# A planned recurrence-plus-MoE kernel: engine choice per operation, output stores in the plan, one-chunk early groups, a third early PSUM bank

## The chip, the cores and the metric

The kernel runs on one core of one Trainium2 chip. The metric is device time in microseconds (us). The kernel before takes 207.4 us (median of 3 runs, 207.34 to 208.5). A profile covers one execution; its span is about 2 us shorter than the device time.

Engine names as in the profile: PE (TensorE, matmuls), PEld (its weight loads), DVE (VectorE), ACT (ScalarE), POOL (GpSimd), SPq (the queue of SyncE, which issues all DMAs here). A "bank" is one buffer of PSUM, the memory that the matmuls write; an "evacuation" copies a result out of its bank, and only then can PE use the bank again. The clock quoted is PE's granted clock, 1.00 being full.

## The reference

```python
# q, k, v, alpha: (4, 8, 768, 48) float32; w_in (384, 2048); w_out (2048, 384)
for t in range(S):                                   # gated linear attention
    state = alpha[:, :, t, :, None] * state + einsum('bhd,bhe->bhde', k[:, :, t], v[:, :, t])
    y[:, :, t] = einsum('bhd,bhde->bhe', q[:, :, t], state)
x = y.transpose(0, 2, 1, 3).reshape(3072, 384)
h = x @ w_in
out = relu(h)**2 @ w_out                             # squared-relu expert layers
```

## The kernel before

The 3072 tokens are 24 chunks of 128. Each chunk goes through a recurrence chain: load alpha, q, k, v; logarithm of alpha on ACT (written to `L_s`); cumulative sums on PE; exponentials on ACT; products on DVE; transposes, scores, masks, output, and a last transpose into `xT_big`. Then come the two expert layers: the first ("ph", 16 column blocks, a relu on ACT, a square on DVE or POOL) and the second ("po", 16 accumulating matmuls a chunk, an evacuation, a store).

Python builds a list of operations with a guessed duration and dependencies, a list scheduler simulates them in time, and the instructions are emitted in the order of the simulated start times. Each engine then executes its own list in that order. The guesses set no time, only the order.

```python
class Op:       # engine, guessed duration, emit function, dependencies, priority, PSUM slot, latency
    ...
def run(self, gate):              # list scheduler; "DMA" is first-in first-out, other engines by (time, prio)
    ...
        op.start = t
        free[eng] = t + op.dur
        op.done = t + op.dur + op.lat
    self.order.sort(key=lambda o: o.start)
...
d["ld_" + nm] = add("DMA", 1.02, ld, prev, lat=2.0)            # 4 loads a chunk
ln = d["use_at"] = add("ACT", 0.41, e_ln, d["ld_at"], old, prio=-5.0)
...
GN = [2] * 12                                                  # chunks per expert group
...
rl = add("ACT", (72 + n) / 1200.0, e_relu, op, prio=-20.0)
eng, nm, dur = (nc.vector, "DVE", ...) if f % 2 == 0 else (nc.gpsimd, "POOL", n / 460.0)   # squares
...
tail = g == NG - 1 and tt % 2 == 1                             # only the last tile uses another bank
ev = add("DVE" if tt % 2 == 0 else "ACT", ...)                 # evacuation
add("OUT", 0.55, e_out, ev)                                    # the store: its own planned engine
...
for op in plan.order:
    op.emit()
```

Loads and stores leave through one SyncE queue, but in the plan a store ("OUT") takes nothing from the loads ("DMA").

Of the kernel before, what the change touches and what calls it, by code (L numbers as in the profile page):

```python
# [8 lines left out]
FP32 = mybir.dt.float32  # L9
# [32 lines left out]
class Plan:  # L42
# [7 lines left out]
    def add(self, op):  # L50
        self.pending.setdefault(op.eng, []).append(op)
        return op

    def ready(self, op):
        t = op.at
        for d in op.deps:
            if d.done is None:
                return None
            t = max(t, d.done)
        if op.takes is not None:  # L60
            f = op.takes.free_at()
            if f is None:
                return None
            t = max(t, f)
        return t

    def run(self, gate):
        free = self.free
        while any(self.pending.values()):
            best = None  # L70
            for eng, ops in self.pending.items():
                t0 = free.get(eng, 0.0)
                pick = None
                fifo = eng in ("DMA",)
                for op in (ops[:1] if fifo else ops):
                    if not gate(op):
                        continue
                    r = self.ready(op)
                    if r is None:
                        continue  # L80
                    key = (max(r, t0), op.prio)
                    if pick is None or key < pick[0]:
                        pick = (key, op)
                if pick is not None and (best is None or pick[0][0] < best[0]):
                    best = (pick[0][0], eng, pick[1])
            assert best is not None, "nothing can run"
            t, eng, op = best
            self.pending[eng].remove(op)
            op.start = t
            free[eng] = t + op.dur  # L90
            op.done = t + op.dur + op.lat
            if op.takes is not None:
                op.takes.release.append(op.gives if op.gives is not None else op)
            self.order.append(op)
            self.on_pick(op)
        self.order.sort(key=lambda o: o.start)
# [3 lines left out]
def kernel(  # L100
# [34 lines left out]
    work = ctx.enter_context(tc.tile_pool(name="work", bufs=4))  # L135
    rpool = ctx.enter_context(tc.tile_pool(name="rpool", bufs=6))
    opool = ctx.enter_context(tc.tile_pool(name="opool", bufs=4))
# [48 lines left out]
    sl_misc, sl_sc, sl_h, sl_o = Slots(2), Slots(1), Slots(2), Slots(1)  # L186
    dma_prev = [None]

# [4 lines left out]
    w_in_ready, w_out_ready = [], []  # L193
    NWP = 4

    def load_w_in(i):
        w = d_ff // NWP
        sl = slice(i * w, (i + 1) * w)
        box = {}

        def ld():
            box["t"] = wload.tile([P, KT * d_ff // NWP], FP32, name="wst").rearrange("p (j n) -> p j n", j=KT)
            nc.sync.dma_start(out=box["t"], in_=w_in_r[:, :, sl])

        d = add("DMA", 2.3, ld, lat=2.0)
        cs = []
        for j in range(KT):
            if j < 2:
                cs.append(add("DVE", 0.34, lambda j=j: pin(nc.vector.tensor_copy(w_in_b[:, j, sl], box["t"][:, j, :])), d, prio=1))
            else:  # L210
                cs.append(add("ACT", 0.62, lambda j=j: pin(nc.scalar.copy(w_in_b[:, j, sl], box["t"][:, j, :])), d, prio=1))
        w_in_ready.append(cs)

    def load_w_out(i):
# [6 lines left out]

        d = add("DMA", 2.3, ld, lat=2.0)
        cs = []
        for j in range(w):
            if j < 3:
                cs.append(add("DVE", 0.26, lambda j=j: pin(nc.vector.tensor_copy(w_out_b[:, i * w + j, :], box["t"][:, j, :])), d, prio=1))
            else:
                cs.append(add("ACT", 0.5, lambda j=j: pin(nc.scalar.copy(w_out_b[:, i * w + j, :], box["t"][:, j, :])), d, prio=1))
        w_out_ready.append(cs)
# [5 lines left out]
    def add_loads(s):  # L235
        d = C[s]
        b, c = divmod(s, NCH)
        for nm, src in srcs:
            def ld(nm=nm, src=src):
                d[nm] = loads.tile([P, H, D], FP32, name=nm)  # L240
                nc.sync.dma_start(out=d[nm], in_=src[b, c])  # L241
            prev = C[s - LB]["use_" + nm] if s >= LB else None
            d["ld_" + nm] = add("DMA", 1.02, ld, prev, lat=2.0)

    def add_chunk(s):
# [18 lines left out]
        def e_p0():  # L264
            pm = d["pm"] = ps_misc.tile([P, 512], FP32, name="misc")
            mm(pm[:, 0:HD], lhsT=utri_b[:, 0, :], rhs=L[:, :, 0:D], start=True, stop=True)
            for p in range(NP):
                mm(pm[:, HD + p:HD + p + 1], lhsT=L[:, 2 * p:2 * p + 2, :], rhs=ones_col,
                   start=True, stop=True)
        p0 = Op("PE", 0.28, e_p0, [ln], takes=sl_misc, **g)  # L270
        p0.gla = s
# [32 lines left out]
        def e_p1():  # L304
# [3 lines left out]
            for p in range(NP):  # L308
                tr(d["pT"][:, NP + p, :], kI[:, 2 * p:2 * p + 2, :], ident_bf)
        p1 = plan.add(Op("PE", 0.47, e_p1, [mq, mk], takes=sl_misc, **g))  # L310

# [6 lines left out]
        def e_p2():  # L318
            sc = d["sc"] = ps_sc.tile([P, 2, NP, P], FP32, name="sc")
            t = d["qkT"]  # L320
            for p in range(NP):
                for hh in range(2):
                    sl = slice(64 * hh, 64 * hh + 64)
                    mm(sc[:, hh, p, :], lhsT=t[sl, NP + p, :], rhs=t[sl, p, :], start=True, stop=True)
        p2 = plan.add(Op("PE", 0.42, e_p2, [cp], takes=sl_sc, **g))

# [32 lines left out]
        def e_p3():  # L359
# [5 lines left out]
            for hh in range(2):  # L365
                for p in range(NP):
                    h = 2 * p + hh
                    mm(py[:, h * D:(h + 1) * D], lhsT=d["sm"][:, hh, p, :], rhs=d["vb"][:, h, :],
                       start=(c == 0 and hh == 0 and p == 0), stop=True, skip_group_check=True)
        p3 = plan.add(Op("PE", 0.39, e_p3, [sm1, vb, C[s - 1]["sb"] if c else None], takes=sl_misc, **g))  # L370

# [6 lines left out]
        def e_p4():  # L378
            d["px"] = ps_misc.tile([P, KT, P], BF16, name="misc")
            for j in range(KT):  # L380
                tr(d["px"][:, j, :], d["xn"][:, j * P:(j + 1) * P], ident_bf)
        p4 = plan.add(Op("PE", 0.18, e_p4, [xn], takes=sl_misc, **g))

        def e_xT():
            pin(nc.vector.tensor_copy(xT_big[:, :, s * P:(s + 1) * P], d["px"]))  # L385
        d["x"] = add("DVE", 0.27, e_xT, p4, prio=-9.0)
        p4.gives = d["x"]
        d["end"] = d["x"]


    GN = [2, 2, 2, 2, 2, 2, 2, 2, 2, 2, 2, 2]
    assert sum(GN) == NT
    GT = [sum(GN[:i]) for i in range(len(GN))]
    NG = len(GN)
    gT = {}
    NQ = 4
    sq = {}
    prog = {"m1": 0.0, "m2": 0.0}

    def add_moe1(g, f, before):  # L400
# [3 lines left out]
        def e_mm():  # L404
            prog_t = ps_h.tile([P, 512], FP32, name="ph")
            box["ph"] = prog_t
# [3 lines left out]
        deps = [C[s]["x"] for s in range(GT[g], GT[g] + GN[g])] + w_in_ready[f * NWP // FT] + [before]  # L410
        op = plan.add(Op("PE", 3 * n / 2400.0 + 0.01, e_mm, deps, takes=sl_h, prio=0.0))
        op.moe = (1, GN[g] * 2.56 / FT)

        def e_relu():
            box["r"] = rpool.tile([P, 512], BF16, name="r")
            pin(nc.scalar.activation(box["r"][:, 0:n], box["ph"][:, 0:n], AF.Relu))  # L416
        rl = add("ACT", (72 + n) / 1200.0, e_relu, op, prio=-20.0)
        op.gives = rl
        eng, nm, dur = (nc.vector, "DVE", 0.05 + n / 1900.0) if f % 2 == 0 else (nc.gpsimd, "POOL", n / 460.0)

        def e_sq():
            if f == 0:
                gT[g] = big.tile([P, FT, 384], BF16, name=f"gT{g % 3}", tag=f"gT{g % 3}")
            pin(eng.tensor_mul(gT[g][:, f, 0:n], box["r"][:, 0:n], box["r"][:, 0:n]))  # L424
        fr = sq[(g - 3, "free")] if g >= 3 else None
        first = sq[(g, 0)] if f else None
        sq[(g, f)] = add(nm, dur, e_sq, rl, fr, first, prio=0.0)
        return op

    def add_moe2(g, tt, before):  # L430
        box = {}
        op = None
        tail = g == NG - 1 and tt % 2 == 1
        for qd in range(NQ):
            def e_mm(qd=qd):
                if qd == 0:
                    box["po"] = (ps_misc.tile([P, 512], FP32, name="misc")[:, 0:d_model] if tail
                                 else ps_o.tile([P, d_model], FP32, name="po"))
                for kf in range(qd * FT // NQ, (qd + 1) * FT // NQ):
                    mm(box["po"], lhsT=gT[g][:, kf, tt * P:(tt + 1) * P], rhs=w_out_b[:, kf, :],  # L440
                       start=(kf == 0), stop=(kf == FT - 1))
            deps = [sq[(g, f)] for f in range(FT)] + sum(w_out_ready, []) + [before if qd == 0 else op]
            op = plan.add(Op("PE", 2.56 / NQ, e_mm, deps, takes=(sl_misc if tail else sl_o) if qd == 0 else None, prio=0.1, lat=0.2))
            op.moe = (2, 2.56 / NQ)
# [5 lines left out]
        def e_ev():  # L450
            box["ob"] = opool.tile([P, d_model], FP32, name="ob")
            if tt % 2 == 0:
                pin(nc.vector.tensor_copy(box["ob"], box["po"]))  # L453
            else:
                pin(nc.scalar.copy(box["ob"], box["po"]))
        ev = add("DVE" if tt % 2 == 0 else "ACT", 0.47 if tt % 2 == 0 else 0.37, e_ev, op, prio=-15.0)
        firstop.gives = ev

        def e_out():
            nc.sync.dma_start(out=out_r[GT[g] + tt], in_=box["ob"])  # L460
        add("OUT", 0.55, e_out, ev)
        return op
# [18 lines left out]

    LEAD = 5

# [15 lines left out]
    for _ in range(9):  # L499
        mm(wp, lhsT=warm[:, 0:P], rhs=warm, start=True, stop=True)  # L500
    for op in plan.order:
        op.emit()

# [28 lines left out]
```

## Time and profile before

| stretch (us) | what happens | how it reads |
|---|---|---|
| 0 to 18 | first loads, chunks 0 and 1, first weights | PE has little to do |
| 18 to 41 | first layer of chunks 0 to 3 | clock low or PE idle |
| 41 to 80 | everything overlaps, loads still arriving | some PE idle |
| 80 to 190 | PE nearly full, full from 100 | a two-chunk group each 14.3 us |
| 190 to 206 | last tiles | two waits for one output bank |

The busy table by stretches of the kernel before: stretch, its length, then busy us and instruction counts of each engine, the granted PE clock (1.00 is full), the mean DMA share, GB/s.

```profile
core 0: us, PE busy (x) PEld busy (x) DVE busy (x) ACT busy (x) POOL busy (x), PEclk, DMA share, GB/s
15.00:25.00 10.00, 7.69 (x51) 4.98 (x49) 5.43 (x15) 6.70 (x18) 2.79 (x5) 0.63 1.02 252
25.00:35.00 10.00, 5.86 (x87) 4.32 (x84) 9.58 (x21) 6.36 (x19) 3.54 (x6) 1.00 1.04 316
35.00:45.00 10.00, 9.04 (x63) 6.16 (x63) 6.35 (x18) 6.67 (x21) 4.06 (x7) 0.83 1.08 215
...
60.00:80.00 20.00, 18.39 (x228) 14.12 (x228) 16.48 (x35) 15.45 (x50) 8.41 (x14) 1.00 1.15 199
100.00:120.00 20.00, 19.95 (x229) 15.12 (x227) 16.10 (x34) 15.08 (x44) 8.04 (x14) 1.00 1.06 198
```

PE is full from 100 us on. Between 15 and 45 us it is either slow (clock 0.63, 0.83) or partly idle (busy 5.86 of 10 us).

The PE timeline of the kernel before, early: start, duration, instruction, count; in brackets the idle time before it and what ended it.

```profile
18.00 5.55 PE L180 MATMUL ph<-xT_big,w_in_b 128*128 128x256 bf16 x27 [0.45 <-DVE xT_big L385]
...
36.00 1.42 PE L180 MATMUL ph<-xT_big,w_in_b 128*128 128x256 bf16 x6 [0.45 <-DVE xT_big L385]
```

27 matmuls in 5.55 us and 6 in 1.42 us are 0.21 to 0.24 us each; 256 columns take 0.109 us later. The second group starts only at 36.0 us, when its second chunk is ready.

The SyncE queue of the kernel before, in its timelines:

```profile
44.56 0.98 SPq L241 DMA_DIRECT2D kt<-in_k_dram  x1
48.73 0.36 SPq L460 DMA_DIRECT2D out_dram<-ob  x1
```

```profile
57.44 0.49 ACT L282 ACTIVATE Ainv<-misc 128x384 bf16<-128x384 f32 x1
59.52 0.52 ACT L255 ACTIVATE L_s<-at 128x384 bf16<-128x384 f32 x1 [1.59 <-DMA at<-in_alpha_dram]
59.95 0.64 ACT L416 ACTIVATE r<-ph 128x256 bf16<-128x256 f32 x2
```

```profile
58.85 0.36 PE L180 MATMUL misc<-vb,sm 128*128 128x48 bf16 x8
60.37 0.49 PE L180 MATMUL ph<-xT_big,w_in_b 128*128 128x256 bf16 x3 [1.15 <-ACT r L416]
```

The first store holds the queue from the last load at 44.56 us to 48.73 us. Some later loads land after ACT is ready for them.

The PE timeline at the tail, where one output bank makes PE wait for each evacuation:

```profile
194.11 2.76 PE L180 MATMUL po<-w_out_b,gT_3360 128*128 128x384 bf16 x16 [0.65 <-DVE ob L453]
197.44 2.76 PE L180 MATMUL po<-w_out_b,gT_3553 128*128 128x384 bf16 x16 [0.57 <-ACT ob L455]
```

### The profile page before, as it was taken

How to read it: one execution, taken by the hardware profiler on the slowest of the kernel's cores; microseconds unless marked ns; L12 is line 12 of the kernel's file. 1: busy time of each engine (PE TensorE's matmuls, PEld its weight loads, DVE VectorE, ACT ScalarE, POOL GpSimd, SP SyncE). 2: the span in 40 equal slices, each digit the busy share in tenths (PEclk: the TensorE clock that was granted, in tenths of full speed). 3: DMA queues.
4: the chain of work that ended last, by engine and by line, in shares of the span. 5: the costliest groups of instructions: out<-in, count | busy, mean ns of one | idle time of the engine just before them, and what ended most of it. 6: DMA issues, size and time to landing. Idle time of an engine off the chain costs nothing.

```text
span 206.1 us, 5137 instructions
## 1 busy us (share of the span) xinstructions
PE 185.6 (90%) x1897; PEld 133.9 (65%) x1897; DVE 140.0 (68%) x294; ACT 130.0 (63%) x377; POOL 76.2 (37%) x133
## 2 busy tenths in 40 slices
PE   7566964999979899999999999999999999999883
PEld 2344643576656687677787777677777777777551
DVE  0684699588769598778968776887787787444210
ACT  3535964676667687777787686677776774655100
POOL 5111550353134535454443444344333333444200
PEclk9855899699999999999999999999999999999999
DMA  7999999996799999999999996410111011100212
GB/s 129 189 356 317 170 281 379 196 197 125 153 213 199 197 216 189 213 178 220 166 225 184 202 216 130 110 38 0 41 38 45 0 41 38 41 16 23 76 41 76
DMA packets 107032, 30.21 MB, mean 147 GB/s; under 512 B 100352, under 2 KB 105472, under 8 KB 107008
## 3 DMA queue, kind: packets, MB, share of 16 engines
q1 hardware_dynamic: 107008, 29.89, 69.7%
q8 instruction: 15, 0.25, 0.5%
q14 instruction: 9, 0.07, 0.1%
HBM read 25.17 MB, written 4.72 MB: 145 GB/s over the span
## 4 chain that ended last, share of the span: by engine, by line
PE 65%; DVE 9%; DMA 8%; ACT 6%; issue 5%; SPq 4%; POOL 2%; POOLq 0%; ACTq 0%; DVEq 0%
PE ph L180 26%; PE po L180 24%; PE misc L180 6%; PE misc L183 5%; DMA wst<-in_moe_w_in_dram 4%; SPq L241 3%; PE sc L180 3%; ACT r L416 3%; DMA at<-in_alpha_dram 2%; DVE qkT L314 2%; DMA vt<-in_v_dram 2%; DVE sm L330 2%; DVE ob L453 1%; DVE xT_big L385 1%; PE st L180 1%
## 5 line engine op out<-in xcount | busy, mean ns | idle before, releaser
L180 PE MATMUL ph<-xT_big,w_in_b 128*128 128x256 bf16 x576 | 84.7, 281 | 4.0 <-ACT r L416 2.8
L416 ACT ACTIVATE r<-ph 128x256 bf16<-128x256 f32 x192 | 68.5, 384 | 29.1 <-PE ph L180 27.6
L180 PEld LDWEIGHTS <-w_in_b 128*128 128x128 bf16 x576 | 53.0, 100 | 18.5 <-issue 6.5
L330 DVE TENSOR_TENSOR sm<-sc,utri_b 128x512 bf16<-128x512 f32 x48 | 31.5, 683 | 1.9 <-PE sc L180 1.4
L261 POOL CAST vb<-vt 128x384 bf16<-128x384 f32 x24 | 13.4, 557 | 29.1 <-DMA vt<-in_v_dram 18.4
L297 DVE TENSOR_TENSOR qA_s<-qt,A 128x384 bf16<-128x384 f32 x24 | 13.6, 570 | 10.8 <-ACT A L278 10.8
L255 ACT ACTIVATE L_s<-at 128x384 bf16<-128x384 f32 x24 | 12.5, 521 | 8.2 <-DMA at<-in_alpha_dram 8.1
L314 DVE COPY qkT<-misc 128x1024 bf16<-128x1024 bf16 x24 | 16.3, 681 | 1.8 <-PE misc L183 1.7
L300 DVE TENSOR_TENSOR kI_s<-kt,Ainv 128x384 bf16<-128x384 f32 x24 | 16.3, 683 | 1.7
L278 ACT ACTIVATE A<-misc 128x384 bf16<-128x384 f32 x24 | 11.6, 489 | 9.1 <-PE misc L180 9.0
L180 PEld LDWEIGHTS <-qkT 64*128 64x128 bf16 (+1 forms) x272 | 11.0, 97 | 8.6 <-DVE qkT L314 5.7
L374 ACT CAST xn<-misc 128x384 bf16<-128x384 f32 x24 | 11.5, 478 | 3.9 <-PE misc L180 3.7
L356 ACT CAST sb<-st 128x384 bf16<-128x384 f32 x20 | 9.5, 476 | 5.2 <-DVE st L351 5.2
L180 PE MATMUL misc<-vb,sm 128*128 128x48 bf16 x192 | 9.5, 186 | 3.5 <-DVE sm L330 3.5
L453 DVE COPY ob<-po 128x384 f32<-128x384 f32 x12 | 6.6, 551 | 8.6 <-PE po L180 8.4
L282 ACT ACTIVATE Ainv<-misc 128x384 bf16<-128x384 f32 x24 | 11.7, 492 | 0.0
L183 PE MATMUL misc<-ident_bf,qA_s 128*128 128x128 bf16 x96 | 9.5, 223 | 2.3 <-DVE qA_s L297 2.2
L180 PE MATMUL sc<-qkT 64*128 64x128 bf16 x192 | 9.8, 223 | 1.5 <-DVE qkT L314 1.1
L351 DVE TENSOR_TENSOR st<-st,ae_s 128x384 f32<-128x384 f32 x20 | 11.0, 552 | 0.0
L180 PEld LDWEIGHTS <-sm 128*128 128x128 bf16 x192 | 7.5, 98 | 4.6 <-DVE sm L330 4.3
L424 POOL TENSOR_TENSOR gT_592<-r 128x256 bf16<-128x256 bf16 x8 | 5.3, 657 | 13.7 <-ACT r L416 13.6
L183 PE MATMUL misc<-ident_bf,kI_s 128*128 128x128 bf16 x96 | 9.5, 223 | 0.8 <-DVE kI_s L300 0.7
(86 smaller groups left out, 321.7 us busy)
## 6 DMA issues: line engine op xcount, KB each, us to landing
at<-in_alpha_dram SPq DMA_DIRECT2D x24, 192.0 KB, 4.6
qt<-in_q_dram SPq DMA_DIRECT2D x24, 192.0 KB, 4.4
kt<-in_k_dram SPq DMA_DIRECT2D x24, 192.0 KB, 4.3
vt<-in_v_dram SPq DMA_DIRECT2D x24, 192.0 KB, 4.3
out_dram<-ob SPq DMA_DIRECT2D x24, 192.0 KB, 1.9
wst<-in_moe_w_in_dram SPq DMA_DIRECT2D x4, 768.0 KB, 8.1
wst<-in_moe_w_out_dram SPq DMA_DIRECT2D x4, 768.0 KB, 7.6
```

The lines of the kernel that those rows point to most:

```text
L180: pin(nc.tensor.matmul(*a, **kw))
L183: pin(nc.tensor.transpose(*a))
L255: pin(nc.scalar.activation(L[:, :, 0:D], d["at"], AF.Ln))
L261: pin(nc.gpsimd.tensor_copy(d["vb"], d["vt"]))
L278: pin(nc.scalar.activation(d["A"], d["pm"][:, 0:HD].rearrange("p (h d) -> p h d", h=H), AF.Exp))
L282: pin(nc.scalar.activation(d["Ai"], d["pm"][:, 0:HD].rearrange("p (h d) -> p h d", h=H), AF.Exp, scale=-1.0))
L297: pin(nc.vector.tensor_mul(qA[:, :, 0:D], d["qt"], d["A"]))
L300: pin(nc.vector.tensor_mul(kI[:, :, 0:D], d["kt"], d["Ai"]))
L314: pin(nc.vector.tensor_copy(d["qkT"], d["pT"]))
L330: pin(nc.vector.tensor_mul(d["sm"][:, hh], d["sc"][:, hh], utri_b.to_broadcast([P, NP, P])))
L374: pin(nc.scalar.copy(d["xn"], d["py"][:, 0:HD]))
L416: pin(nc.scalar.activation(box["r"][:, 0:n], box["ph"][:, 0:n], AF.Relu))
```

## The change

The intent: squares, weight casts and evacuations go to whichever engine the plan finds free; stores are charged to the loads in the plan and emitted 1.5 us late; chunks 2 and 3 are groups of their own, so that first-layer work starts earlier; early first-layer work may use the idle output bank; the last two groups alternate output banks; filler matmuls on zeros keep the PE clock up in planned gaps.

```diff
     def add(self, op):
-        self.pending.setdefault(op.eng, []).append(op)
+        op.durs = op.eng if isinstance(op.eng, dict) else {op.eng: op.dur}
+        for e in op.durs:
+            self.pending.setdefault(e, []).append(op)
...
-            op.start = t
+            op.start = t + getattr(op, "late", 0.0)
             free[eng] = t + op.dur
+            if eng == "OUT":
+                free["DMA"] = max(free.get("DMA", 0.0), t) + op.dur
...  # casts: DVE or ACT by index -> {"DVE": ..., "POOL": ...}; relu ring 6 -> 8 buffers; load guess 1.02 -> 1.08
...  # weight-load guess 2.3 -> 2.2; planned latency of xT_big +0.3; relu priority of groups 0 and 1: -20 -> 0
-    GN = [2, 2, 2, 2, 2, 2, 2, 2, 2, 2, 2, 2]
+    GN = [2, 1, 1, 2, 2, 2, 2, 2, 2, 2, 2, 2, 2]
+    M1_ALT = 3
+    OUT_LATE = 1.5
...
-        op = plan.add(Op("PE", ..., takes=sl_h, prio=0.0))
+        op = plan.add(Op("PE", ..., takes=[sl_h, sl_o] if g < M1_ALT else [sl_h], prio=0.0))
-        sq[(g, f)] = add(nm, dur, e_sq, rl, fr, first, prio=0.0)
+        sq[(g, f)] = add({"DVE": 0.05 + n / 1900.0, "POOL": 0.06 + n / 440.0}, 0, e_sq, rl, fr, first, prio=SQ_PRIO)
-        tail = g == NG - 1 and tt % 2 == 1
+        tail = g >= NG - 2                       # and takes=[sl_o, sl_misc]
-        ev = add("DVE" if tt % 2 == 0 else "ACT", ...)
+        ev = add({"DVE": 0.47, "ACT": 0.37}, 0, e_ev, op, prio=-15.0)
-        add("OUT", 0.55, e_out, ev)
+        add("OUT", 0.55, e_out, ev, at=0.0).late = OUT_LATE
-    LEAD = 5
+    LEAD = 4
...
+            if pe_end is not None and DUMMY:     # only before the first second-layer matmul
+                n = max(0, int((op.start - pe_end - 0.5) / 0.22))
+                for _ in range(n):
+                    mm(wp, lhsT=warm[:, 0:P], rhs=warm, start=True, stop=True)
```

More of the change, by code (lines that the diff above doesn't have):

```diff
@@ L60, in ready @@
         if op.takes is not None:
-            f = op.takes.free_at()
-            if f is None:
+            best = None
+            for sl in op.takes:
+                f = sl.free_at()
+                if f is not None and (best is None or f < best):
+                    best, op.slot = f, sl
+            if best is None:
                 return None
-            t = max(t, f)
+            t = max(t, best)
         return t
@@ L87, in run @@
             t, eng, op = best
-            self.pending[eng].remove(op)
-            op.start = t
+            for e in op.durs:
+                self.pending[e].remove(op)
+            op.eng, op.dur = eng, op.durs[eng]
+            op.start = t + getattr(op, "late", 0.0)
             free[eng] = t + op.dur
+            if eng == "OUT":
+                free["DMA"] = max(free.get("DMA", 0.0), t) + op.dur
             op.done = t + op.dur + op.lat
             if op.takes is not None:
-                op.takes.release.append(op.gives if op.gives is not None else op)
+                self.ready(op)
+                op.slot.release.append(op.gives if op.gives is not None else op)
             self.order.append(op)
@@ L135 @@
     work = ctx.enter_context(tc.tile_pool(name="work", bufs=4))
-    rpool = ctx.enter_context(tc.tile_pool(name="rpool", bufs=6))
+    rpool = ctx.enter_context(tc.tile_pool(name="rpool", bufs=8))
     opool = ctx.enter_context(tc.tile_pool(name="opool", bufs=4))
@@ L186 @@
     sl_misc, sl_sc, sl_h, sl_o = Slots(2), Slots(1), Slots(2), Slots(1)
-    dma_prev = [None]
+    X_SLACK = 0.3
+    LD = 1.08
+    WLD = 2.2
+    SQ_PRIO = 0.0
     def add(eng, dur, emit, *deps, **kw):
@@ L194, with cast, e_cast @@
     NWP = 4
+    def cast(dst, box, j, d, n):
+        def e_cast():
+            eng = nc.vector if op.eng == "DVE" else nc.gpsimd
+            pin(eng.tensor_copy(dst, box["t"][:, j, :]))
+        op = add({"DVE": 0.06 + n / 1840.0, "POOL": 0.05 + n / 660.0}, 0, e_cast, d, prio=1.0)
+        return op
     def load_w_in(i):
@@ L203, in ld @@
             nc.sync.dma_start(out=box["t"], in_=w_in_r[:, :, sl])
-        d = add("DMA", 2.3, ld, lat=2.0)
+        d = add("DMA", WLD, ld, lat=2.0)
         cs = []
         for j in range(KT):
-            if j < 2:
-                cs.append(add("DVE", 0.34, lambda j=j: pin(nc.vector.tensor_copy(w_in_b[:, j, sl], box["t"][:, j, :])), d, prio=1))
-            else:
-                cs.append(add("ACT", 0.62, lambda j=j: pin(nc.scalar.copy(w_in_b[:, j, sl], box["t"][:, j, :])), d, prio=1))
+            cs.append(cast(w_in_b[:, j, sl], box, j, d, 512))
         w_in_ready.append(cs)
@@ L220, in ld @@
             nc.sync.dma_start(out=box["t"], in_=w_out_r[:, i * w:(i + 1) * w, :])
-        d = add("DMA", 2.3, ld, lat=2.0)
+        d = add("DMA", WLD, ld, lat=2.0)
         cs = []
         for j in range(w):
-            if j < 3:
-                cs.append(add("DVE", 0.26, lambda j=j: pin(nc.vector.tensor_copy(w_out_b[:, i * w + j, :], box["t"][:, j, :])), d, prio=1))
-            else:
-                cs.append(add("ACT", 0.5, lambda j=j: pin(nc.scalar.copy(w_out_b[:, i * w + j, :], box["t"][:, j, :])), d, prio=1))
+            cs.append(cast(w_out_b[:, i * w + j, :], box, j, d, d_model))
         w_out_ready.append(cs)
@@ L242, in add_loads @@
             prev = C[s - LB]["use_" + nm] if s >= LB else None
-            d["ld_" + nm] = add("DMA", 1.02, ld, prev, lat=2.0)
+            d["ld_" + nm] = add("DMA", LD, ld, prev, lat=2.0, at=0.6)
     def add_chunk(s):
@@ L269, in e_p0 @@
                    start=True, stop=True)
-        p0 = Op("PE", 0.28, e_p0, [ln], takes=sl_misc, **g)
+        p0 = Op("PE", 0.28, e_p0, [ln], takes=[sl_misc], **g)
         p0.gla = s
@@ L309, in e_p1 @@
                 tr(d["pT"][:, NP + p, :], kI[:, 2 * p:2 * p + 2, :], ident_bf)
-        p1 = plan.add(Op("PE", 0.47, e_p1, [mq, mk], takes=sl_misc, **g))
+        p1 = plan.add(Op("PE", 0.47, e_p1, [mq, mk], takes=[sl_misc], **g))
         def e_cp():
@@ L324, in e_p2 @@
                     mm(sc[:, hh, p, :], lhsT=t[sl, NP + p, :], rhs=t[sl, p, :], start=True, stop=True)
-        p2 = plan.add(Op("PE", 0.42, e_p2, [cp], takes=sl_sc, **g))
+        p2 = plan.add(Op("PE", 0.42, e_p2, [cp], takes=[sl_sc], **g))
         def e_sm(hh):
@@ L369, in e_p3 @@
                        start=(c == 0 and hh == 0 and p == 0), stop=True, skip_group_check=True)
-        p3 = plan.add(Op("PE", 0.39, e_p3, [sm1, vb, C[s - 1]["sb"] if c else None], takes=sl_misc, **g))
+        p3 = plan.add(Op("PE", 0.39, e_p3, [sm1, vb, C[s - 1]["sb"] if c else None], takes=[sl_misc], **g))
         def e_xn():
@@ L381, in e_p4 @@
                 tr(d["px"][:, j, :], d["xn"][:, j * P:(j + 1) * P], ident_bf)
-        p4 = plan.add(Op("PE", 0.18, e_p4, [xn], takes=sl_misc, **g))
+        p4 = plan.add(Op("PE", 0.18, e_p4, [xn], takes=[sl_misc], **g))
         def e_xT():
             pin(nc.vector.tensor_copy(xT_big[:, :, s * P:(s + 1) * P], d["px"]))
-        d["x"] = add("DVE", 0.27, e_xT, p4, prio=-9.0)
+        d["x"] = add("DVE", 0.27, e_xT, p4, prio=-9.0, lat=0.2 + X_SLACK)
         p4.gives = d["x"]
         d["end"] = d["x"]
-    GN = [2, 2, 2, 2, 2, 2, 2, 2, 2, 2, 2, 2]
+    GN = [2, 1, 1, 2, 2, 2, 2, 2, 2, 2, 2, 2, 2]
     assert sum(GN) == NT
@@ L396 @@
     NQ = 4
+    M1_ALT = 3
+    OUT_LATE = 1.5
+    RELU_PRIO = -20.0
+    RELU_PRIO0 = 0.0
+    DUMMY = 1
     sq = {}
@@ L404, in e_mm @@
         def e_mm():
-            prog_t = ps_h.tile([P, 512], FP32, name="ph")
+            prog_t = (ps_o.tile([P, 512], FP32, name="po") if op.slot is sl_o
+                      else ps_h.tile([P, 512], FP32, name="ph"))
             box["ph"] = prog_t
@@ L410, in add_moe1 @@
         deps = [C[s]["x"] for s in range(GT[g], GT[g] + GN[g])] + w_in_ready[f * NWP // FT] + [before]
-        op = plan.add(Op("PE", 3 * n / 2400.0 + 0.01, e_mm, deps, takes=sl_h, prio=0.0))
+        op = plan.add(Op("PE", 3 * n / 2400.0 + 0.01, e_mm, deps, takes=[sl_h, sl_o] if g < M1_ALT else [sl_h], prio=0.0))
         op.moe = (1, GN[g] * 2.56 / FT)
@@ L416, in e_relu @@
             pin(nc.scalar.activation(box["r"][:, 0:n], box["ph"][:, 0:n], AF.Relu))
-        rl = add("ACT", (72 + n) / 1200.0, e_relu, op, prio=-20.0)
+        rl = add("ACT", (72 + n) / 1200.0, e_relu, op, prio=RELU_PRIO if g > 1 else RELU_PRIO0)
         op.gives = rl
-        eng, nm, dur = (nc.vector, "DVE", 0.05 + n / 1900.0) if f % 2 == 0 else (nc.gpsimd, "POOL", n / 460.0)
         def e_sq():
@@ L423, in e_sq @@
                 gT[g] = big.tile([P, FT, 384], BF16, name=f"gT{g % 3}", tag=f"gT{g % 3}")
+            eng = nc.vector if sq[(g, f)].eng == "DVE" else nc.gpsimd
             pin(eng.tensor_mul(gT[g][:, f, 0:n], box["r"][:, 0:n], box["r"][:, 0:n]))
@@ L432, in add_moe2, with e_mm @@
         op = None
-        tail = g == NG - 1 and tt % 2 == 1
+        tail = g >= NG - 2
         for qd in range(NQ):
-            def e_mm(qd=qd):
+            def e_mm(qd=qd, me=None):
                 if qd == 0:
-                    box["po"] = (ps_misc.tile([P, 512], FP32, name="misc")[:, 0:d_model] if tail
-                                 else ps_o.tile([P, d_model], FP32, name="po"))
+                    box["po"] = (ps_o.tile([P, 512], FP32, name="po") if firstop.slot is sl_o
+                                 else ps_misc.tile([P, 512], FP32, name="misc"))[:, 0:d_model]
                 for kf in range(qd * FT // NQ, (qd + 1) * FT // NQ):
@@ L442, in add_moe2 @@
             deps = [sq[(g, f)] for f in range(FT)] + sum(w_out_ready, []) + [before if qd == 0 else op]
-            op = plan.add(Op("PE", 2.56 / NQ, e_mm, deps, takes=(sl_misc if tail else sl_o) if qd == 0 else None, prio=0.1, lat=0.2))
+            op = plan.add(Op("PE", 2.56 / NQ, e_mm, deps, takes=([sl_o, sl_misc] if tail else [sl_o]) if qd == 0 else None, prio=0.1, lat=0.2))
             op.moe = (2, 2.56 / NQ)
@@ L451, in e_ev @@
             box["ob"] = opool.tile([P, d_model], FP32, name="ob")
-            if tt % 2 == 0:
+            if ev.eng == "DVE":
                 pin(nc.vector.tensor_copy(box["ob"], box["po"]))
@@ L455, in e_ev @@
                 pin(nc.scalar.copy(box["ob"], box["po"]))
-        ev = add("DVE" if tt % 2 == 0 else "ACT", 0.47 if tt % 2 == 0 else 0.37, e_ev, op, prio=-15.0)
+        ev = add({"DVE": 0.47, "ACT": 0.37}, 0, e_ev, op, prio=-15.0)
         firstop.gives = ev
@@ L500 @@
         mm(wp, lhsT=warm[:, 0:P], rhs=warm, start=True, stop=True)
+    pe_end = None
     for op in plan.order:
+        if op.eng == "PE":
+            if getattr(op, "moe", (0,))[0] == 2:
+                pe_end = None
+                DUMMY = 0
+            if pe_end is not None and DUMMY:
+                n = max(0, int((op.start - pe_end - 0.5) / 0.22))
+                if n:
+                    wp = ps_o.tile([P, 512], FP32, name="po")
+                for _ in range(n):
+                    mm(wp, lhsT=warm[:, 0:P], rhs=warm, start=True, stop=True)
+            pe_end = op.start + op.dur
         op.emit()
```

## The prediction

> **What bounds it now.** The busy table by stretches shows TensorE (PE) saturated from 60 to 190 us (19.9 of 20 us busy between 100 and 180, granted clock 1.00). The timeline gives one group of two chunks every 14.3 us there, so twelve groups need about 172 us of the 206.1 us span. The other 34 us are the start and the tail:
> - 0 to 18 us: loads, two recurrence chunks and weight casts; the first expert-input matmul starts at 18.0 us.
> - 18 to 41 us: PE idles 4.1 us between 25 and 35 us, and the second group waits for both its chunks until 36.0 us. The clock is 0.63 in 15 to 25 us and 0.83 in 35 to 45 us: a 128x256 matmul takes about 0.21 us at 18 to 23 and 36 to 40 us, 0.109 us later. The Trainium skill ("TensorE: Matmul & The Clock Gate", Part 1) says an idle PE falls to half rate and sustained activity restores it; these numbers agree.
> - 41 to 80 us: about 4 us of slack. The SyncE queue stands from 44.56 to 48.73 us, the first output store holding back input loads behind it.
> - Tail: PE stands 0.65 and 0.57 us for the one output bank, then evacuation and store.
>
> **What the change does.**
> 1. Single-chunk groups for chunks 2 and 3: first-layer work starts when chunk 2 is ready (estimate 31 to 33 us), not at 36.0. A 128-column matmul costs about 55 ns (four transposes in 0.22 us), so the halved width costs PE nothing.
> 2. 31 filler matmuls (0.215 us warm, 0.43 cold, estimates from the columns) in planned gaps before the second layer, to raise the clock. Up to 5 us of slow-clock loss is there, but much turns into waiting for chunks 2 and 3 and for the second weights (cast until about 40 us). Fillers may overrun by 0.3 to 0.5 us.
> 3. Eight weight casts (0.5 to 0.6 us) leave ACT: the one at 16.0 us no longer delays chunk 1's evacuation, 0.5 us.
> 4. A third PSUM bank for early first-layer work removes waits of 0.2 us each.
> 5. Squares go from 96 DVE / 96 POOL to 84 / 124; evacuations mostly to ACT. In steady state PE hides these. The skill ("GPSIMD Engine Reference", Key points) says GpSimd shares its SBUF interfaces with VectorE; here a DVE square takes 0.29 us alone, 0.53 us beside POOL's. POOL rises to about 9 of 14.3 us per group.
> 6. Stores are placed later against their data: the 4.2 us queue stall should shrink to about 1 us.
> 7. Tail: output tiles alternate banks: 1.2 us.
>
> **On the critical path.** At 40 us I expect PE ahead by about 3.3 us of work (first layer of chunks 0 to 3 done, where before about 20 of the second group's 48 matmuls were). Steps 4 and 6 give 1 us between 41 and 80 us, the tail 1.2 us. As PE is saturated afterwards, the lead survives. Sum 5.5 us.
>
> **Prediction: 201.9 us, range 198.5 to 206.0. Chances: faster by over 2% 0.65, within 2% 0.31, slower 0.04.**
>
> **What would show it.** Right: clock near 1.0 in 15 to 25 and 35 to 45 us; first 128-wide matmul by 33 us; first second-layer matmul at about 40 us; group period still 14.3 us; no bank wait in the tail. Wrong: cold matmuls still there; fillers ahead of ready work; PE waiting on POOL; a period above 14.5 us.
>
> **What would make it wrong.** Fillers in PE's in-order stream delaying chains 0 to 3; input loads, which fill the DMA until about 125 us, starving the earlier PE; slow POOL casts holding the second weights; or a warm clock gaining more than I allow.

## The result, and the profile after

The change takes 200.84 us (median of 4 runs, 200.57 to 201.7) against 207.37 us; the ratio is 0.968, 95% interval 0.9636 to 0.9724. A ratio here is the mean time of one kernel's fast runs over that of the other's fast runs of the same rounds, so it is not quite the ratio of the medians quoted.

The same stretches after:

```profile
core 0: us, PE busy (x) PEld busy (x) DVE busy (x) ACT busy (x) POOL busy (x), PEclk, DMA share, GB/s
15.00:25.00 10.00, 8.26 (x62) 6.00 (x62) 7.12 (x17) 5.94 (x17) 5.33 (x8) 0.83 1.02 254
25.00:35.00 10.00, 8.10 (x101) 5.38 (x101) 8.50 (x20) 5.72 (x21) 4.83 (x10) 1.00 1.09 316
35.00:45.00 10.00, 9.11 (x114) 6.81 (x111) 8.63 (x30) 7.30 (x32) 6.27 (x14) 1.00 1.08 199
...
60.00:80.00 20.00, 19.19 (x237) 15.41 (x235) 17.82 (x37) 17.69 (x53) 13.57 (x21) 1.00 1.11 190
100.00:120.00 20.00, 20.00 (x231) 15.27 (x229) 13.60 (x26) 15.06 (x46) 12.23 (x21) 1.00 1.03 195
```

35 to 45 us is now at full clock; 15 to 25 us only partly (0.83). Between 25 and 35 us PE is busier (8.10 against 5.86), but that is the fillers, ten of them there: the needed work is 4.5 us against 4.8 before (sums as explained below). POOL is at about 12 of 20 us.

The PE timeline after, early, and what DVE does just before the second layer starts:

```profile
17.62 1.33 PE L191 MATMUL ph<-xT_big,w_in_b 128*128 128x256 bf16 x6 [1.34 <-DVE xT_big L400]
...
32.34 0.34 PE L191 MATMUL ph<-xT_big,w_in_b 128*128 128x128 bf16 x3
...
38.20 0.33 PE L191 MATMUL po<-xT_big,w_in_b 128*128 128x128 bf16 x3
38.37 0.56 PE L191 MATMUL ph<-xT_big,w_in_b 128*128 128x128 bf16 x6
38.89 0.33 PE L191 MATMUL po<-xT_big,w_in_b 128*128 128x128 bf16 x3
...
41.84 0.32 PE L191 MATMUL misc<-L_s,utri_b 128*128 128x384 bf16 x1 [0.48 <-ACT L_s L270]
...
42.10 2.76 PE L191 MATMUL po<-w_out_b,gT_340 128*128 128x384 bf16 x16
```

```profile
38.91 1.78 DVE L444 TENSOR_TENSOR gT_752<-r 128x128 bf16<-128x128 bf16 x5
40.61 0.35 DVE L213 CAST w_out_b<-wst 128x384 bf16<-128x384 f32 x1
...
41.42 0.35 DVE L213 CAST w_out_b<-wst 128x384 bf16<-128x384 f32 x1
```

The first 128-column matmul comes at 32.34 us. The second layer comes at 42.10 us, **later** than the 41.31 us of before and than the 40 us I expected. Until 41.2 us PE still runs chunk 3's first layer, which stands before it in PE's order. Three tiles of it (nine matmuls) start every 0.7 us, from 38.20 us on, where nine warm 128-column matmuls need 0.50 us: this is the pace of ACT's relus, which empty the banks (three of them start in 0.7 us too). Then PE waits 0.48 us, until 41.84 us, for a logarithm. The last second-weight cast, on DVE between squares, ends at 41.77 us, so it alone would have held the second layer about as long.

ACT and the SyncE queue after, at the place of the 1.59 us wait:

```profile
58.49 0.38 ACT L437 ACTIVATE r<-ph 128x256 bf16<-128x256 f32 x1 [0.21 <-PE ph L191]
...
60.17 0.54 ACT L270 ACTIVATE L_s<-at 128x384 bf16<-128x384 f32 x1
```

```profile
41.94 0.95 SPq L256 DMA_DIRECT2D vt<-in_v_dram  x1
45.40 0.36 SPq L480 DMA_DIRECT2D out_dram<-ob  x1
...
54.63 0.69 SPq L256 DMA_DIRECT2D at<-in_alpha_dram  x1
```

Chunk 8's logarithm now stands behind the relus (60.17 us) and waits for nothing. Its load was issued at 54.63 us, where the kernel before issued it at 55.59 us, but landed at 59.42 us against 59.50 us: no sooner. And the first store still holds the queue, from 41.94 to 45.40 us.

The tail after has no bracket, so PE never waits for the bank:

```profile
186.76 3.41 PE L191 MATMUL misc<-w_out_b,gT_3487 128*128 128x384 bf16 x20
190.01 2.76 PE L191 MATMUL po<-w_out_b,gT_3721 128*128 128x384 bf16 x16
192.61 2.76 PE L191 MATMUL misc<-w_out_b,gT_3721 128*128 128x384 bf16 x16
```

To see where the lead comes from I added up the *needed* PE work that each trace has done by a time: each matmul at its warm cost as the timelines space them (256 columns 0.109 us, 384 0.1635, 128 0.0556, 96 0.042, 48 and 1 0.026), fillers left out, a running one in proportion. The 64-row score matmuls are counted as 128 columns. These sums are worked out from the traces, one profile each (all needed matmuls, 1888 before and 1936 after, are recorded), and differences below about 0.3 us mean little. Each matmul is counted once. An earlier sum counted those at the edges of 15 us windows twice, 2.2 to 2.4 us too many by 190 us; the recorded expectations below still quote it.

```
us of needed PE work done by time t
t (us)                40     55     70     80    100    190
before              14.51  28.21  40.30  49.83  68.80 157.88
after               16.98  30.47  44.13  53.97  73.88 163.83
lead                 2.47   2.26   3.83   4.14   5.08   5.95
```

About 2.5 us of lead exist by 40 us, 1.6 more appear between 55 and 70 us, 0.9 between 80 and 100 us, 0.9 between 100 and 190 us, and the tail adds about 1.3 (the spans differ by 7.3 us).

### The profile page after: what moved, and what is told of

Its sections match the earlier page's. It is cut to its first block, busy times and chain, and to the rows that moved or that the text cites. A ratio compares the mean times of both kernels' runs of the same rounds, so it can differ in the third digit from the quotient of the medians.

```text
span 198.8 us, 5351 instructions
## 1 busy us (share of the span) xinstructions
PE 186.3 (94%) x1973; PEld 136.1 (68%) x1976; DVE 130.3 (66%) x265; ACT 131.8 (66%) x396; POOL 101.5 (51%) x175
## 4 chain that ended last, share of the span: by engine, by line
PE 78%; ACT 5%; DVE 5%; DMA 4%; SPq 4%; issue 2%; POOL 2%; ACTq 0%; POOLq 0%; DVEq 0%
PE po L191 29%; PE ph L191 28%; PE misc L191 10%; PE misc L194 6%; DMA wst<-in_moe_w_in_dram 4%; PE sc L191 4%; SPq L256 3%; ACT r L437 3%; PE st L191 1%; DVE gT_606 L444 1%; DVE w_out_b L213 1%; DVE gT_752 L444 1%; POOL gT_340 L444 1%; DVE qkT L329 1%; POOL gT_1148 L444 1%
## 5 line engine op out<-in xcount | busy, mean ns | idle before, releaser
L437 ACT ACTIVATE r<-ph 128x256 bf16<-128x256 f32 (+1 forms) x192 | 67.5, 374 | 30.7 <-PE ph L191 25.9
L191 PE MATMUL ph<-xT_big,w_in_b 128*128 128x256 bf16 (+1 forms) x576 | 81.6, 269 | 2.4 <-DVE xT_big L400 1.3
L191 PEld LDWEIGHTS <-w_in_b 128*128 128x128 bf16 x624 | 54.1, 99 | 17.3 <-issue 3.6
L475 ACT COPY ob<-po 128x384 f32<-128x384 f32 x20 | 9.6, 478 | 6.6 <-PE po L191 6.2
L400 DVE COPY xT_big<-misc 128x384 bf16<-128x384 bf16 x24 | 8.5, 354 | 8.1 <-PE misc L194 8.0
L191 PE MATMUL po<-warm 128*128 128x512 bf16 x37 | 10.9, 424 | 1.6 <-DVE ae_s L184 1.3
L444 POOL TENSOR_TENSOR gT_3206<-r 128x256 bf16<-128x256 bf16 x12 | 7.6, 639 | 6.2 <-ACT r L437 5.3
L444 POOL TENSOR_TENSOR gT_2317<-r 128x256 bf16<-128x256 bf16 x12 | 7.6, 639 | 5.7 <-ACT r L437 4.8
L444 POOL TENSOR_TENSOR gT_2008<-r 128x256 bf16<-128x256 bf16 x12 | 7.6, 639 | 5.6 <-ACT r L437 4.9
L444 POOL TENSOR_TENSOR gT_2923<-r 128x256 bf16<-128x256 bf16 x12 | 7.6, 642 | 5.5 <-ACT r L437 5.0
```

Source lines behind the costliest of these rows:

```text
L191: pin(nc.tensor.matmul(*a, **kw))
L437: pin(nc.scalar.activation(box["r"][:, 0:n], box["ph"][:, 0:n], AF.Relu))
L444: pin(eng.tensor_mul(gT[g][:, f, 0:n], box["r"][:, 0:n], box["r"][:, 0:n]))
```

## The experiments

Single parts of the change are undone ("undone" rows), or one part is put into the kernel before. Control: the change itself again, in the rounds of e14, e16 and e17 below; the six runs of the table stood in other rounds, so all are compared through the kernel before, which ran in every round.

> Control: the change itself beside these three on one chip. All theories: ratio 0.968 to the kernel before, about 200.8.

It gave 200.45 us, ratio 0.9688 (0.9651 to 0.9725). I take 0.9684, the mean of the two ratios, as the change's, and turn a ratio r into a cost as (r − 0.9684) × 207.4 us.

| run | what it is | median us | ratio (95%) | cost of undoing, us |
|---|---|---|---|---|
| e4_out_old | old store model | 203.65 | 0.9824 (0.9765 to 0.9884) | 2.9 |
| e6_tail_old | old tail | 201.89 | 0.9751 (0.9694 to 0.9807) | 1.4 |
| e1_no_filler | no fillers | 201.27 | 0.9726 (0.9647 to 0.9804) | 0.9 |
| e2_pairs | chunks 2, 3 as a pair | 201.45 | 0.9721 (0.9669 to 0.9774) | 0.8 |
| e7_two_banks | no third bank | 201.28 | 0.9690 (0.9656 to 0.9724) | 0.1 |
| e8_fixed_all | engines fixed | 200.13 | 0.9644 (0.9600 to 0.9689) | −0.8 |

An interval is 0.7 to 1.6 us to each side. The six costs add up to 5.3 us of the 6.5. The profiled spans, one execution each, say much the same: 2.4, 1.4, 0.8, 0.5, 0.6 and −0.2 us longer than the change's 198.8 us, in the order of the table. What was never undone: LEAD (how many chunks the recurrence may run ahead, 5 to 4), the relu ring, the new guesses for loads and latency, and the relu priority. Only the store model is clear of the control's interval by time alone; the tail is supported by its trace; the other four are within noise.

### Without fillers

```diff
-    DUMMY = 1
+    DUMMY = 0
```

> The change without its 31 filler matmuls. Theory A (the gain is earlier work, a better order after 41 us and the tail; the warm clock only turns into waiting for chunks 2 and 3 and the second weights): 0.3 to 1.5 us slower than the change (200.84), so 201.1 to 202.3, though the mean clock drops from 0.991 towards 0.96. Theory B (the warm clock is the main gain): 3 to 5 us slower, 204 to 206, with first-layer matmuls of chunks 2 and 3 at half rate.

It was 201.27 us (0.9 us by ratio, within noise). Its stretches, and then the first of the control's:

```profile
15.00:25.00 10.00, 8.66 (x60) 6.43 (x60) 6.37 (x17) 5.85 (x17) 4.71 (x7) 0.65 1.08 252
25.00:35.00 10.00, 6.91 (x82) 5.45 (x80) 8.37 (x19) 5.43 (x19) 4.43 (x9) 0.69 1.06 325
```

```profile
15.00:25.00 10.00, 7.74 (x72) 5.78 (x72) 8.48 (x20) 6.49 (x19) 5.68 (x8) 1.00 1.06 263
```

The clock is 0.65 and 0.69 without fillers. The same changed kernel had 0.83 at 15 to 25 us in its first profile and 1.00 in the control's. That warmer profile had 1.4 us more work done by 22 us (7.63 against 6.19) but only 0.2 us more by 40 us (17.21 against 16.98), and its span is 198.5 against 198.8 us. So the warm clock there turns almost wholly into waiting, as theory A says; theory B, the clock as the main gain (3 to 5 us), falls: the interval allows 2.5 us at most.

### Chunks 2 and 3 as a pair

```diff
-    GN = [2, 1, 1, 2, ...]        M1_ALT = 3
+    GN = [2, 2, 2, ...]           M1_ALT = 2
```

> The change with chunks 2 and 3 as one group of two again (third bank kept for chunks 0 to 3). The work curves of the two traces show a lead of 2.3 us appearing between 30 and 40 us. Theory A: the single-chunk groups make it, so 1.5 to 3 us slower than the change, 202.3 to 203.8. Theory B: with the clock kept warm by the fillers the pair is done nearly as early, 0 to 1 us slower.

201.45 us, a cost of 0.8 us: below theory A's 1.5 to 3, inside theory B's 0 to 1. The work curve says why: at 40 us it is 1.15 us behind the change (15.83 against 16.98), at 70 us level with it (43.99 against 44.13). The early lead of the singles is mostly not kept. What holds the change back there I did not isolate.

### The old store model

```diff
-            if eng == "OUT":
-                free["DMA"] = max(free.get("DMA", 0.0), t) + op.dur
-    OUT_LATE = 1.5
+    OUT_LATE = 0.0
```

> The change with the output stores modelled as before (no charge to the loads, no lateness), so that they stand earlier in the SyncE queue. The lead grows by 1.7 us between 55 and 65 us and 1.2 us between 80 and 100 us. Theory A: part of it comes from the stores no longer holding back loads, so 0.5 to 2 us slower, 201.3 to 202.8. Rival: loads are far enough ahead, within 0.4 us.

203.65 us, 2.9 us of the whole 6.5: more than any theory expected. Two things are undone at once and were not tested apart: the lateness moves only the stores' own places in the queue, the charge moves whatever the plan times by its loads. The run is level with the change until 55 us (30.52 against 30.47) and then loses 2.1 us by 70 us (42.05 against 44.13). Its queue, ACT and PE there:

```profile
54.70 0.69 SPq L254 DMA_DIRECT2D at<-in_alpha_dram  x1
```

```profile
57.74 0.48 ACT L295 ACTIVATE Ainv<-misc 128x384 bf16<-128x384 f32 x1
59.86 0.52 ACT L268 ACTIVATE L_s<-at 128x384 bf16<-128x384 f32 x1 [1.63 <-DMA at<-in_alpha_dram]
60.29 0.64 ACT L435 ACTIVATE r<-ph 128x256 bf16<-128x256 f32 x2
```

```profile
60.70 0.82 PE L189 MATMUL ph<-xT_big,w_in_b 128*128 128x256 bf16 x6 [1.19 <-ACT r L435]
```

The alpha load of chunk 8 is issued at 54.70 us, as in the change (54.63), and lands at 59.77 us (59.42 in the change). But the logarithm stands in front of the relus again, waits 1.63 us, and PE waits 1.19 us: the picture of the kernel before. So this load comes at nearly the same time in all three kernels; its user is placed differently. That was theory C, and it needed a test with the queue order held.

### Moving the logarithms alone

First all of them, from chunk 6 on, after planning:

```diff
     plan.run(gate)
+    p0s = {...}                                                       # start of each logarithm's first user
+    for s in range(6, NT):
+        ln = C[s]["use_at"]
+        ln.start = max(ln.start, min(p0s[s] - 1.2, ln.start + 3.0))
+    plan.order.sort(key=lambda o: o.start)
```

> The kernel with the old store model (e4_out_old, 203.65, ratio 0.982), in which only the logarithms of chunks 6 and later move later in ACT's queue (by at most 3 us, never past 1.2 us before their first user); the SyncE queue, TensorE, VectorE and GpSimd keep their orders. Theory C (the store model pays because a logarithm that waits for a late alpha load no longer stands in ACT's in-order queue ahead of relus that TensorE needs): most of the loss of about 3 us comes back, ratio 0.970 to 0.975, and no logarithm after 45 us waits more than 0.3 us for its load while relus stand behind it. Rival D (the order of loads and stores on the SyncE queue, or the DMA's share, is what pays): stays at 0.980 to 0.984.

> The kernel before with the same move of the logarithms in ACT's queue and nothing else. There the trace shows logarithms waiting 1.03, 1.59, 0.66 and 1.11 us for alpha loads between 54 and 69 us, and PE waiting 1.15 and 0.64 us for the relus behind them. Theory C: 1.5 to 3 us faster than the kernel before, ratio 0.986 to 0.993. Rival D: within 0.5 us, 0.997 to 1.003.

e16 (old store model): 203.20 us, ratio 0.9804 (0.9775 to 0.9833). By time that is rival D's value. By the work curve it is mixed: from 55 to 65 us it did 9.31 us of work (e4_out_old 7.98, the change 9.35), and from 100 to 160 us 58.45 (e4_out_old 59.97). By 55 us it was already 1.1 us behind e4_out_old, with a clock of 0.84 in 25 to 35 us where that had 1.00; the profiled execution was its slowest, 204.09 us. Moving every logarithm cured the stall and cost as much later, so the edit was too coarse to decide. e17 (the kernel before): 206.55 us, ratio 0.9978 (0.9946 to 1.0011): less than theory C's 1.5 to 3 us and inside rival D's range. Its profile, of its fastest execution, was 1.45 us ahead at 80 us (51.28 against 49.83) and 1.6 us ahead at 190. It is no clean test either: chunk 9's logarithm still waits 1.45 us for its load there, and PE 1.16 us for that logarithm.

Then one instruction only, chunk 8's logarithm, in the kernel with the old store model. The instruction lists of all other engines are unchanged:

```diff
     plan.run(gate)
+    C[8]["use_at"].start += 2.6
+    plan.order.sort(key=lambda o: o.start)
```

> The old-store-model kernel (203.65, ratio 0.982) with one instruction moved: chunk 8's logarithm goes behind nine others in ACT's queue; all other engines' orders are unchanged. Moving all logarithms (e16_ln_late) brought back 1.6 us between 55 and 65 us and lost 1.9 us between 100 and 160 us. Theory C (the logarithm that waits 1.63 us for its load blocks the relus behind it): 1.0 to 2.0 us faster than e4_out_old, ratio 0.972 to 0.978; the PE wait of about 1.2 us near 60 us is gone. Rival D (only the order of loads and stores counts): 0.980 to 0.984.

202.65 us, ratio 0.9758 (0.9720 to 0.9795), within theory C's range; the intervals of the two kernels overlap, so the trace has to carry it. ACT and PE:

```profile
60.82 0.54 ACT L268 ACTIVATE L_s<-at 128x384 bf16<-128x384 f32 x1
...
68.09 0.52 ACT L268 ACTIVATE L_s<-at 128x384 bf16<-128x384 f32 x1 [1.00 <-DMA at<-in_alpha_dram]
...
77.19 0.52 ACT L268 ACTIVATE L_s<-at 128x384 bf16<-128x384 f32 x1 [1.22 <-DMA at<-in_alpha_dram]
```

```profile
78.42 0.49 PE L189 MATMUL ph<-xT_big,w_in_b 128*128 128x256 bf16 x3 [0.99 <-ACT r L435]
```

Chunk 8's logarithm now waits for nothing and the 1.19 us wait is gone: 13.12 us of work from 55 to 70 us, against 11.53 in e4_out_old and 13.66 in the change. But the later logarithms, which had not waited there, now do (1.00, 1.22 us), PE waits again (0.99 us at 78.42), and from 70 to 80 us it does 8.14 us against 9.61. So one blocked logarithm costs about 1.6 us where it stands, and curing it alone exposes the next ones, which take 1.5 us back: over the whole profile 0.3 us is left (span 200.9 against 201.2 us). As I read it, the old plan's whole timetable of loads is too early, not one entry. By time, theory C and rival D stay undecided: e16 and e17 came out at D's values, e18 at C's, with overlapping intervals.

### The store model alone in the kernel before

```diff
-            op.start = t
+            op.start = t + getattr(op, "late", 0.0)
+            if eng == "OUT":
+                free["DMA"] = max(free.get("DMA", 0.0), t) + op.dur
-    add("OUT", 0.55, e_out, ev)
+    add("OUT", 0.55, e_out, ev).late = 1.5
-    rpool ... bufs=6
+    rpool ... bufs=8
```

With six relu buffers this order does not build: it deadlocks. With eight it does.

> The kernel before with only the change's store model (a store is charged to the loads and placed 1.5 us late) and 8 relu buffers, since with 6 it does not build (deadlock). If the store model works by itself, 2 to 3.5 us faster than before, ratio 0.983 to 0.990; if it needs the other parts (engine choice, retuned load and weight costs), less than 1 us.

It was **slower**: 210.71 us, ratio 1.0179 (1.0139 to 1.0219), against both expectations. By 80 us it was 2.6 us ahead of the kernel before (52.44 against 49.83), as hoped; then it lost. One stall is the same kind, on ACT and PE:

```profile
90.86 0.52 ACT L257 ACTIVATE L_s<-at 128x384 bf16<-128x384 f32 x1 [1.80 <-DMA at<-in_alpha_dram]
```

```profile
91.71 0.82 PE L182 MATMUL ph<-xT_big,w_in_b 128*128 128x256 bf16 x6 [1.87 <-ACT r L418]
```

From 100 to 180 us it did 76.59 us of work, the kernel before 79.43. No single wait in its trace explains that part, and I did not isolate it. Its tail then has four waits for the output bank (0.65, 0.56, 0.65 and 0.61 us) where the kernel before has two. So the store model pays within the change's other settings (load guess 1.08, lead 4, groups, tail) and not by itself; which of these it needs stays open.

### Old tail, fixed engines, two banks

```diff
-        tail = g >= NG - 2                              # takes [sl_o, sl_misc]
+        tail = g == NG - 1 and tt % 2 == 1              # takes [sl_misc]
```

> The change with the old tail: one output bank but for the very last tile. Theory A: two waits of about 0.6 us return before the last tiles, 1.0 to 1.5 us slower, 201.8 to 202.3, and PE shows them as waits for an evacuation. Rival: the first of them hides, 0.3 to 0.7 us.

201.89 us, 1.4 us by ratio. Its PE timeline has the two waits back, 1.14 us together:

```profile
188.02 2.76 PE L191 MATMUL po<-w_out_b,gT 128*128 128x384 bf16 x16 [0.57 <-ACT ob L475]
191.35 2.76 PE L191 MATMUL po<-w_out_b,gT 128*128 128x384 bf16 x16 [0.57 <-ACT ob L475]
```

```diff
-        {"DVE": ..., "POOL": ...}  squares, casts;  {"DVE": 0.47, "ACT": 0.37}  evacuations
+        squares: f % 2;  casts: DVE for the first pieces, else ACT;  evacuations: (GT[g] + tt) % 2
```

> The change with squares, weight casts and evacuations each tied to the engine of the kernel before (the rest of the change kept). As predicted: PE hides squares and evacuations in steady state, casts are worth about 0.5 us: 0.3 to 1.0 us slower than the change, ratio 0.970 to 0.974. Rival (free engine choice is needed for the plan to hold, as the failure of the store model alone in the kernel before suggests): over 2 us slower, ratio above 0.978.

200.13 us, ratio 0.9644 (0.9600 to 0.9689): not slower at all. The intervals overlap, so I do not call it faster. The part of the change that stands first in its description is worth nothing measurable, and the casts' 0.5 us is not there either: chunk 1's evacuation is back at 16.77 us, and yet as much work is done by 40 us (17.08 us against 16.98).

```diff
-    M1_ALT = 3
+    M1_ALT = 0
```

> The change without the third PSUM bank for early first-layer work. As predicted (it removes waits of 0.2 us each, and the one-chunk groups run at the pace of their evacuation): 0.5 to 1.5 us slower than the change, ratio 0.971 to 0.976. Rival (the early work waits for loads and second weights anyway): within 0.4 us.

201.28 us, ratio 0.9690: the rival's value, though the interval (0.7 us to each side) reaches into the first theory's. Its PE timeline shows what the bank does: without it only two tiles (six matmuls) start every 0.7 us, each pair behind a relu, where the change starts three.

```profile
38.66 0.56 PE L191 MATMUL ph<-xT_big,w_in_b 128*128 128x128 bf16 x6 [0.20 <-ACT r L437]
39.42 0.50 PE L191 MATMUL ph<-xT_big,w_in_b 128*128 128x128 bf16 x6 [0.20 <-ACT r L437]
```

The trace is 0.9 us of work behind the change at 55 us (29.61 against 30.47) and still 0.8 us at 190 us (163.07 against 163.83). So this one profile keeps what the bank gives early, the times show 0.1 us, and between the two the runs do not decide.

### An attempt to go further

```diff
-    GN = [2, 1, 1, 2, ...]          M1_ALT = 3    LEAD = 4
+    GN = [2, 1, 1, 1, 1, 2, ...]    M1_ALT = 4    LEAD = 4.5
```

> An attempt to beat the change: chunks 4 and 5 are single too, the third bank serves one group more, the lead of the recurrence is 4.5 chunks. If the early groups still gain by starting sooner: 0.3 to 1.0 us faster than the change, ratio 0.963 to 0.967. If the lead made by 45 us is set by loads and second weights: no difference, 0.967 to 0.971.

200.96 us, ratio 0.9676 (0.9636 to 0.9716): no difference. No run beat the change clearly.

## Why the prediction was right or wrong, point by point

The time (201.9 predicted, 200.84 measured) and the direction were right. The terms of the sum were less so, and that the total came so close is partly luck: by the work sums the part before 40 us brought 0.8 us less than predicted (2.5 for 3.3), 40 to 80 us brought 0.7 us more (1.7 for 1), and 80 to 190 us brought 1.8 us where none was predicted.

- **What bounds the kernel: right.** From 100 us on PE is full in both (from 80 us in the change; before, 19.55 of 20 us between 80 and 100). Three group periods took 42.25 us after (first-layer starts at 107.97 and 150.22 us) and 42.73 us before (112.63 and 155.36), so 14.1 and 14.2 us each, and the lead is kept to the end.
- **Single-chunk groups, "ahead by about 3.3 us" at 40 us: too large.** The lead was 2.5 us. The first 128-column matmul came when expected (32.34 us), but at 40 us nearly five of chunk 3's sixteen tiles were still to run, the missing 0.8 us. The halved width did cost PE something: at 128 columns it was held to the pace of ACT's relus, 0.7 us for three tiles instead of 0.5. So the second layer came at 42.1, not 40 us. Undoing the groups cost only 0.8 us: by 70 us the pairs are level.
- **Fillers: half right.** In the first profile the clock rose fully in 35 to 45 us and only partly in 15 to 25 us. That the warm clock mostly becomes waiting was right and is shown by two profiles of the same kernel.
- **"Eight weight casts leave ACT ... 0.5 us": wrong as a gain.** The evacuation of chunk 1 did start earlier (15.19 us against 16.53), but with the engines fixed again the time is no worse.
- **Squares and evacuations hidden: right.** POOL rose to about 12 of 20 us, which is 8.7 of 14.3, as estimated.
- **Stores, "the 4.2 us queue stall should shrink to about 1 us" and "Steps 4 and 6 give 1 us": the step that failed.** The queue still stood 3.5 us from the last load's issue to the first store (41.94 to 45.40; before 44.56 to 48.73). The part was worth 2.9 us all the same, the largest of all, and by another road: charging the stores moves the planned arrival of later loads, and so the place of their users in in-order queues. The Trainium skill ("TensorE: Matmul & The Clock Gate", Part 1, "Engine queue depths") says ACT and DVE are strict first-in first-out; the trace agrees, with relus standing 1.63 us behind a logarithm that waits for its load. That one logarithm's place costs 1.6 us on the spot is shown by the trace of e18_ln8, though its run kept little of it; that the retimed users explain the whole 2.9 us is argued from the traces, not shown by any run.
- **Tail, 1.2 us: right** (1.4 by ratio, 1.14 us of waits).
- **The third bank's share of that 1 us: open** (0.1 us by ratio, 0.8 us of work at 190 us in one profile). Its waits of 0.2 us are there without it, as predicted.

## What to carry to other kernels

Where a static plan decides the order, a queue that the plan forgets to charge makes every load look early, and an instruction whose load is late then blocks an in-order engine in front of ready work: look for waits on a DMA on an engine that feeds the bottleneck, and if the load's issue has not moved, mend the place of its user. An early lead on the bottleneck need not last: the 1.15 us that the single chunks gave at 40 us was gone at 70 us. A part that pays inside one set of settings may lose in another, so undo parts from the final kernel and also add them to the old one.

## What the Trainium skill lacked or had wrong

- "TensorE: Matmul & The Clock Gate", "Back-to-back issue gap": it gives about 81 ns a matmul at 128 columns and 131 ns at 512 for a stream in which each matmul has its own weight load. Here four 128-column transposes, each with its own weights, start every 0.22 us (55 ns each), 256 columns take 109 ns, and four of 384 take 0.65 us (163 ns each), so 512 columns at 131 ns does not fit.
- "GPSIMD Engine Reference", Key points: it says that GpSimd and VectorE contend for SBUF with two SBUF inputs, but gives no size. In the kernel before, a 128x256 bf16 square on DVE took 0.28 to 0.29 us alone and 0.53 us (median) while POOL worked, and POOL's took 0.61 us.
- "TensorE: Matmul & The Clock Gate", Part 1: it describes a clock window that runs free of the kernel, so that warm-up varies by run. Two profiles of one kernel agree (0.83 and 1.00 in 15 to 25 us). It puts the cost of the ramp at under 1% of a typical kernel's span; it lacks how that fades on a chain that waits for loads: here 1.4 us of work at 22 us, 0.2 us at 40 us of a span of 199 us.
- No page gives the cost of one instruction with a late load in an in-order engine's queue: here 1.63 us on ACT became 1.19 us on PE.
